# Fused attention and two MoE layers on one core: the low halves of one weight set move from DVE to GpSimd, and nine priorities of the planner change

## Chip, cores and metric

One core of a Trainium2 chip. The metric is the time of one launch in device microseconds, the median of several runs. Engines are named as the profile names them: PE (TensorE) multiplies matrices, DVE (VectorE), ACT (ScalarE) and POOL (GpSimd) work elementwise, SP (SyncE) issues most DMAs.

## What is computed

Three pieces in a row, all float32 (the reference, cut):

```
# q, k, v: (4, 8, 576, 64)
out_d  = softmax(pooled q . pooled k) @ pooled v        # means over 4 tokens
local  = softmax(q . k within |i - j| < 4) @ v
x      = (repeat(out_d, 4) + local) as (2304, 512)
h  = x @ w_in;   x = (h * sigmoid(h)) @ w_out           # layer 1: 512 -> 2048 -> 512
h2 = x @ w_in2;  r = max(h2, 0)
out = (s * r * r + b) @ w_out2                          # layer 2: 512 -> 2048 -> 512
```

## The kernel before

Everything is written as operations handed to a list scheduler (class `Weave`). Each has an engine (or a choice of ACT or DVE, `EITHER`), a planned cost in us, the buffers it reads and writes, and a priority `pr` (smaller goes first). `plan` walks through planned time and, on each engine, takes the ready operation with the smallest `pr`; the result is a fixed order for each engine, with semaphores between them. Costs and priorities are numbers at the top of the file (`P_...`), so a number can change the order of all engines that have not yet been planned.

Every float32 factor is split for PE into a high half (a rounded copy, type fp32r) and a low half (the rest, value minus high half); a product is high x high + high x low + low x high.

Layer 2 uses a scheme with seven products of half-size blocks for four block products. In its second half (`out_group`) the hidden activations g come back from memory (`graw`, loaded by `g_load` as four tiles of 128x1024 for each group of 256 tokens; nine groups, p = 0 to 8). `mix` (L1263, DVE) forms sums of these tiles (`gs`), `parted` makes the high half on ACT (`gh`, L1267) and the low half on DVE (`gl`, L1268). The products of a group are b11, t1, t2, b21, t3, t4, b22, in banks oa, oc, oa, ob, oa, ob, oc. Each has eight matmuls 128x512 with the high half of g against both halves of the weight (L1286) and eight 128x256 with the low half (L1293). `snap` copies a piece of the bank with ACT (L1304), and `plus` and `join` add on DVE (`os`, L1301); after them a bank is free for its next product.

There are four weight sets for it: wb (for b11), wt12 (t1 and t2), wout (b21 and b22) and wt43 (t4 and t3). The trace shows wt12 and wt43 both as `wt`. Each has eight parts of 128x512 (wb of 128x256). `in_place` brings a part: SP loads it into the place of the low half (by the helper `dma`, L364 in the trace), ACT or DVE copies it rounded to the place of the high half (L351), and DVE subtracts the high half from it in place (L1226). Sets and the first two groups are interleaved by the string `PAIR`; groups 0 and 1 run together while the weights still arrive, all later groups find them there.

The last block's g is made just before by `late` (`g2`, L1134 on DVE, L1139 on ACT), stored by SP, and read back for the last group.

Of the kernel before, what the change touches and what calls it, by code (L numbers as in the profile page):

```python
# [8 lines left out]
F32 = mybir.dt.float32  # L9
# [4 lines left out]
ALU = mybir.AluOpType  # L14
# [30 lines left out]
MORE = 0.0  # L45
# [1 line left out]
NEARLY = 0  # L47
MASKED = False
ADDED = False
P_IN, P_OUT, P_Y0, P_W0, P_Y1, P_Y4, P_W, P_OS = 163.074, 237.937, 195.038, -36.246, 62.462, 102.369, 272.176, 169.42  # L50
P_STEP, P_BT, P_PO, P_PN = 6.074, -5.7, 16.567, 57.528
P_G, P_B, P_C = -45.097, 0.253, -5.619
D1, D1S = 8, 2
NWARM = 100
ACTW, ACTW2 = 0, True
# [3 lines left out]
NLAST, LASTS = 3, [0, 1, 2]  # L59
VPE, QKPE = 0, 0  # L60
GPV, GPQ, GPS, GPM = 0, 0, 0, 0
PAIR = "AAAAAAAATTTTTTTTG0H101OOOO01OOOO01FFFFFFFF01I0101"
FILL0, FILLG, FILLD = 5.0, 0.12, 0.85
SLOW = 1.05
# [31 lines left out]
class Weave:  # L96
# [9 lines left out]
    def op(self, eng, cost, fn, w=(), r=(), pr=0.0, table=None):  # L106
        n, deps = len(self.ops), set()
        r = [x if isinstance(x, tuple) else (x, None) for x in r]
        w = [x if isinstance(x, tuple) else (x, None) for x in w]

        def hits(d, k):
            return [v for kk, v in d.items() if k is None or kk is None or kk == k]

        for b, k in r:
            deps.update(hits(b.wr, k))
        for b, k in w:
            deps.update(hits(b.wr, k))
            for v in hits(b.rd, k):
                deps.update(v)
        for b, k in r:  # L120
            b.rd.setdefault(k, []).append(n)
        for b, k in w:
            if k is None:
                b.wr, b.rd = {}, {}
            else:
                b.rd.pop(k, None)
            b.wr[k] = n
        deps.discard(n)
        bufs = []
        for b, _ in r + w:  # L130
            if b not in bufs:
                bufs.append(b)
                if not b.left and b.kind in self.turns:
                    self.turns[b.kind].append(b)
                b.left += 1
        self.ops.append((eng if isinstance(eng, tuple) else (eng,), cost, fn, sorted(deps), bufs, pr, table))
        return n
# [133 lines left out]
def dve(n, c=1):  # L271
    return c * 0.07 + n / 960.0


def act(n, c=1):
    return c * 0.1 + n / 1200.0
# [15 lines left out]
def kernel(ctx, tc, q, k, v, w1_in, w1_out, w2_in, w2_out, s2, b2, cst, out):  # L292
    nc = tc.nc
# [41 lines left out]
    op = W.op  # L335
# [13 lines left out]
    def copy(eng, out, in_, by=1.0):  # L349
        if by == 1.0:  # L350
            (nc.scalar.copy if eng == "act" else nc.vector.tensor_copy)(out=out, in_=in_)  # L351
        elif eng == "act":
            nc.scalar.mul(out=out, in_=in_, mul=by)
        else:
            nc.vector.tensor_scalar(out=out, in0=in_, scalar1=by, scalar2=None, op0=ALU.mult)
# [7 lines left out]
    def dma(out, in_, eng=None, **kw):  # L363
        (eng or nc.sync).dma_start(out=out, in_=in_, **kw)  # L364
# [671 lines left out]
    HF = KF // 2  # L1036
# [185 lines left out]
    def in_place(nm, q, o, i, key, n, move, pr):  # L1222
        at = lambda x: o[:, x, i:i + n // P]
        op("sp", (1, move), lambda: dma(at(1).bitcast(F32), w_dram[nm][q][:, :n // P]), w=[(o, key)], r=[(w_dram[nm], q), final], pr=pr)
        op(EITHER, (act(n) + MORE, 0.07 + n / 1920.0 + MORE), lambda eng: copy(eng, at(0), at(1).bitcast(F32)), w=[(o, key)], pr=pr)
        op("dve", dve(n) + MORE, lambda: nc.vector.tensor_tensor(out=at(1), in0=at(1).bitcast(F32), in1=at(0).bitcast(F32), op=ALU.subtract), w=[(o, key)], pr=pr - 0.001)  # L1226

    def ahead(pr):
        for q in range(HF):
            if q % 2 == 0:  # L1230
                o = Buf("u2", [P, 2, KD, P], F32R, "wb")
            in_place("out", q, o, 2 * (q % 2), q % 2, 2 * P, 0.57, pr + 0.1 * q)
            piece_of("b11", q, o, q % 2, q % 2)
            yield

    def named(nm, names, at, pr):
        for q in range(HF):
            o = Buf("u2", [P, 2, KD, P], F32R, "w" + nm)
            in_place(nm, q + at, o, 0, None, DM, 0.88, pr + 0.1 * q)
            for i, name in enumerate(names):  # L1240
                piece_of(name, q, o, i)
            yield
# [103 lines left out]
    def put(o, r0, e=None):  # L1346
# [11 lines left out]
        for by, mine in (("sp", parts_),) if e != 1 else (("sp", parts_[::2]), ("act", parts_[1::2])):  # L1358
# [6 lines left out]
            "F": named("t43", ("t4", "t3"), 0, P_B + 3 * P_C), "0": lead[0], "1": lead[1]}  # L1365
    for x in PAIR:
        if x in "GHI":
# [57 lines left out]
```

## Time and profile before

| what | us |
|---|---|
| three runs | 861.50, 862.49, 863.54 |
| median | 862.49 |
| the profiled execution | 861.29 |
| its span | 859.4 |
| PE busy | 850.0 |
| DVE busy | 734.1 |
| ACT busy | 507.7 |
| POOL busy | 0.2 |

All times of rows are from the profiled execution, from the start of its span. Busy time of a group is its records laid over each other, so eight neighbours whose records overlap show as one row that is shorter than eight times the mean.

### The profile page before, as it was taken

How to read it: one execution, taken by the hardware profiler on the slowest of the kernel's cores; microseconds unless marked ns; L12 is line 12 of the kernel's file. 1: busy time of each engine (PE TensorE's matmuls, PEld its weight loads, DVE VectorE, ACT ScalarE, POOL GpSimd, SP SyncE). 2: the span in 40 equal slices, each digit the busy share in tenths (PEclk: the TensorE clock that was granted, in tenths of full speed). 3: DMA queues.
4: the chain of work that ended last, by engine and by line, in shares of the span. 5: the costliest groups of instructions: out<-in, count | busy, mean ns of one | idle time of the engine just before them, and what ended most of it. 6: DMA issues, size and time to landing. Idle time of an engine off the chain costs nothing.

```text
span 859.4 us, 14697 instructions
## 1 busy us (share of the span) xinstructions
PE 850.0 (99%) x5300; PEld 714.5 (83%) x5300; DVE 734.1 (85%) x1364; ACT 507.7 (59%) x1034; POOL 0.2 (0%) x4
## 2 busy tenths in 40 slices
PE   9999999999999999999999999999999999999998
PEld 8878777778778878888889988888888988888887
DVE  7999996999999999987667788777787999888894
ACT  6998797656456742454456566666666665444351
POOL 0000000000000000000000000000000000000000
PEclk9999999999999999999999999999999999999999
DMA  8995421642444221388985246666679866443311
GB/s 217 319 351 151 132 68 41 191 130 70 106 127 112 77 69 39 123 278 304 330 297 176 86 119 212 205 189 183 184 248 286 274 183 213 160 143 125 123 33 42
DMA packets 157426, 144.26 MB, mean 168 GB/s; under 512 B 65452, under 2 KB 125738, under 8 KB 157354
## 3 DMA queue, kind: packets, MB, share of 16 engines
q1 hardware_dynamic: 156946, 142.96, 53.2%
q8 instruction: 42, 0.69, 0.3%
q10 hardware_dynamic: 408, 0.36, 0.1%
q14 instruction: 30, 0.25, 0.1%
HBM read 102.40 MB, written 40.89 MB: 167 GB/s over the span
## 4 chain that ended last, share of the span: by engine, by line
PE 87%; DVE 7%; ACT 2%; DMA 2%; issue 1%; SPq 0%; ACTq 0%; DVEq 0%
PE hp L926 23%; PE y L926 20%; PE ha L926 10%; PE oa L1286 6%; PE hc L926 5%; PE oc L1286 4%; PE ob L1286 4%; PE oa L1293 3%; PE hb L926 2%; PE oc L1293 2%; PE ob L1293 2%; PE pS L703 1%; DMA wo_raw<-in_moe_w_out_dram 1%; PE pB L842 1%; PE pU L742 1%
## 5 line engine op out<-in xcount | busy, mean ns | idle before, releaser
L926 PE MATMUL hp<-xh,wi 128*128 128x512 f32 (+1 forms) x640 | 200.8, 377 | 0.3 <-ACT g L951 0.3
L926 PE MATMUL y<-gh,wo 128*128 128x512 f32 (+1 forms) x640 | 199.8, 375 | 0.0
L926 PEld LDWEIGHTS hp<-xh,wi 128*128 128x128 f32 x640 | 116.9, 188 | 23.3 <-ACT g L951 2.8
L926 PEld LDWEIGHTS y<-gh,wo 128*128 128x128 f32 x640 | 117.0, 189 | 19.9 <-issue 0.8
L926 PE MATMUL y<-gl,wo 128*128 128x512 f32 (+1 forms) x320 | 118.2, 369 | 0.0
L926 PE MATMUL hp<-xl,wi 128*128 128x512 f32 (+1 forms) x320 | 118.0, 369 | 0.0
L926 PE MATMUL ha<-yh,wi 128*128 128x512 f32 x256 | 86.4, 390 | 0.8 <-ACT g L351 0.8
L952 ACT CAST gh<-g 128x512 fp32r<-128x512 f32 (+1 forms) x80 | 46.2, 577 | 54.2 <-PE y L926 53.3
L951 ACT ACTIVATE g<-hp 128x512 f32<-128x512 f32 (+1 forms) x80 | 44.4, 555 | 41.4 <-DVE gl L953 36.3
L926 PEld LDWEIGHTS y<-gl,wo 128*128 128x128 f32 x320 | 60.4, 189 | 8.7 <-DVE gl L953 0.2
L926 PEld LDWEIGHTS hp<-xl,wi 128*128 128x128 f32 x320 | 60.4, 189 | 8.1
L1139 ACT ACTIVATE g<-g,sbt 128x512 f32<-128x512 f32 (+1 forms) x70 | 53.4, 769 | 23.2 <-DVE g L1134 22.8
L953 DVE TENSOR_TENSOR gl<-g,gh 128x512 fp32r<-128x512 f32 (+1 forms) x80 | 50.5, 631 | 14.5 <-ACT gh L952 14.4
L1134 DVE SCALAR_TENSOR_TENSOR g<-g 128x512 f32<-128x512 f32 (+1 forms) x80 | 49.8, 633 | 9.8 <-ACT g L1133 9.1
L926 PEld LDWEIGHTS ha<-yh,wi 128*128 128x128 f32 x256 | 48.1, 188 | 10.9 <-ACT g L351 1.3
L1267 ACT CAST gh<-gs 128x1024 fp32r<-128x1024 f32 x27 | 28.4, 1052 | 46.7 <-DVE gs L1263 38.7
L1267 ACT CAST gh<-graw 128x1024 fp32r<-128x1024 f32 x36 | 37.6, 1051 | 27.7 <-PE ob L1293 11.6
L926 PE MATMUL ha<-yl,wi 128*128 128x512 f32 x128 | 50.0, 390 | 0.0
L1268 DVE TENSOR_TENSOR gl<-graw,gh 128x1024 fp32r<-128x1024 f32 x36 | 43.6, 1217 | 6.8 <-PE oa L1286 4.1
L351 ACT COPY g<-ha 128x512 f32<-128x512 f32 x48 | 28.1, 585 | 28.0 <-PE ha L926 23.8
L926 PE MATMUL hc<-yh,wi 128*128 128x512 f32 x128 | 44.6, 389 | 0.0
L543 DVE TENSOR_TENSOR tmp<-le,lv 128x1344 f32<-128x1344 f32 (+1 forms) x28 | 37.9, 1353 | 0.5
(197 smaller groups left out, 1721.1 us busy)
## 6 DMA issues: line engine op xcount, KB each, us to landing
graw<-gd SPq DMA_DIRECT2D x36, 512.0 KB
gd<-g SPq DMA_DIRECT2D x64, 256.0 KB
wi_raw<-in_moe_w_in_dram SPq DMA_DIRECT2D x16, 512.0 KB
wo_raw<-in_moe_w_out_dram SPq DMA_DIRECT2D x16, 512.0 KB
w_raw<-in_moe_w_in_dram SPq DMA_DIRECT2D x16, 512.0 KB
w_raw<-in_moe_w_out_dram SPq DMA_DIRECT2D x16, 512.0 KB
nq<-in_q_dram SPq DMA_DIRECT2D x32, 144.0 KB
nk<-in_k_dram SPq DMA_DIRECT2D x32, 144.0 KB
```

The lines of the kernel that those rows point to most:

```text
L351: (nc.scalar.copy if eng == "act" else nc.vector.tensor_copy)(out=out, in_=in_)
L543: op("dve", dve(n * WIN * D), lambda t=t, i0=i0, n=n, h2=h2: nc.vector.tensor_tensor(out=t[:], in0=wide(e[:, h2 * ns + i0:h2 * ns + i0 + n ...
L926: nc.tensor.matmul(t(), lhsT=lhs(i), rhs=rhs(i), start=(first and i == 0), stop=(last and i == 2), **kw)
L951: op("act", act(n), lambda g=g, hp=hp: nc.scalar.activation(out=g[:], in_=hp[:], func=AF.Silu), w=[g], r=[hp], pr=-5, table="silu")
L952: op("act", act(n), lambda g=g, gh=gh: nc.scalar.copy(out=gh[:], in_=g[:]), w=[gh], r=[g], pr=-5)
L953: op("dve", dve(n), lambda g=g, gh=gh, gl=gl: nc.vector.tensor_tensor(out=gl[:], in0=g[:], in1=gh[:].bitcast(F32), op=ALU.subtract), w=[gl ...
L1134: op("dve", dve(n) + 1.5 * MORE, lambda: nc.vector.scalar_tensor_tensor(out=t[:], in0=t[:], scalar=0.0, in1=t[:], op0=ALU.max, op1=ALU.mul ...
L1139: nc.scalar.activation(out=t[:], in_=t[:], func=AF.Identity, scale=sbt[:, 0:1], bias=sbt[:, 1:2])
L1267: op("act", act(HF * P) + MORE, lambda: nc.scalar.copy(out=flat(hi), in_=flat(x)), w=[hi], r=[x], pr=pr + n)
L1268: op("dve", dve(HF * P) + MORE, lambda: nc.vector.tensor_tensor(out=flat(lo), in0=flat(x), in1=flat(hi).bitcast(F32), op=ALU.subtract), w= ...
L1286: nc.tensor.matmul(bank[:].rearrange("p x n -> p (x n)"), lhsT=hi[:, q], rhs=w(), start=new and q == 0, stop=False, skip_group_check=True)
L1293: nc.tensor.matmul(bank[:, 0], lhsT=lo[:, q], rhs=w()[:, 0], start=False, stop=q == HF - 1, skip_group_check=True)
```

## The change

The subtraction of `in_place` goes to GpSimd for a set's last GPT or GPO parts (t43 has GPT = 8 of 8 parts, wout none), with a planned cost of 1.35 us in place of DVE's. Nine priorities have other numbers.

```
-P_IN, P_OUT, P_Y0, P_W0, P_Y1, P_Y4, P_W, P_OS = 163.074, 237.937, 195.038, -36.246, 62.462, 102.369, 272.176, 169.42
+P_IN, P_OUT, P_Y0, P_W0, P_Y1, P_Y4, P_W, P_OS = 163.074, 237.937, 279.61, -80.654, 26.32, 107.348, 404.271, 125.36
...
-P_G, P_B, P_C = -45.097, 0.253, -5.619
+P_G, P_B, P_C = -175.262, -5.511, 0.133
...
+GPT, GPO = 8, 0
...
-        op("dve", dve(n) + MORE, lambda: nc.vector.tensor_tensor(out=at(1), in0=at(1).bitcast(F32), in1=at(0).bitcast(F32), op=ALU.subtract), w=[(o, key)], pr=pr - 0.001)
+        aside = q % HF >= HF - {"t43": GPT, "out": GPO if move > 0.6 else 0}.get(nm, 0)
+        by, engine = ("pool", nc.gpsimd) if aside else ("dve", nc.vector)
+        op(by, 1.35 if aside else dve(n) + MORE, lambda: engine.tensor_tensor(out=at(1), in0=at(1).bitcast(F32), in1=at(0).bitcast(F32), op=ALU.subtract),
+           w=[(o, key)], pr=pr - 0.001)
```

The order of all engines is the same up to the load of wb on SP (some 632 us); the 4900 matmuls and the DMAs are the same in number. Lines of the changed kernel lie 1 higher from L59 on and 4 higher behind `in_place`, so L1226 is now L1229, L1268 is L1272, L1301 is L1305, L1286 is L1290.

DVE before, where wt43 is split (names carry buffer numbers; 128x1024 rows are `gl`, low halves of g):

```order
L1226 TENSOR_TENSOR wout_7796<-wout_7796 128x512
L1268 TENSOR_TENSOR gl_7828<-graw_7497,gh_7818 128x1024
L1268 TENSOR_TENSOR gl_7841<-graw_7557,gh_7830 128x1024
L1226 TENSOR_TENSOR wt43_7843<-wt43_7843 128x512
L1226 TENSOR_TENSOR wt43_7845<-wt43_7845 128x512
...
L1226 TENSOR_TENSOR wt43_7862<-wt43_7862 128x512
L1301 TENSOR_TENSOR os_7758<-oa_7727,os_7758 128x256
L1301 TENSOR_TENSOR os_7758<-ob_7884,os_7758 128x256
L1268 TENSOR_TENSOR gl_7919<-graw_7502,gh_7875 128x1024
L1301 TENSOR_TENSOR os_7758<-ob_7884,os_7758 128x256
L1301 TENSOR_TENSOR os_7784<-oa_7754,os_7784 128x256
```

Here the eight wt43 rows stand in one piece between two `gl` and the adds. The changed kernel's DVE at the same place:

```order
L1272 TENSOR_TENSOR gl_7808<-graw_7497,gh_7798 128x1024
L1305 TENSOR_TENSOR os_7782<-oa_7755,os_7782 128x256
L1272 TENSOR_TENSOR gl_7824<-graw_7557,gh_7813 128x1024
L1267 TENSOR_TENSOR gs_7670<-graw_7557,gs_7670 128x1024
L1229 TENSOR_TENSOR wout_7790<-wout_7790 128x512
L1229 TENSOR_TENSOR wout_7792<-wout_7792 128x512
L1229 TENSOR_TENSOR wout_7794<-wout_7794 128x512
L1272 TENSOR_TENSOR gl_7880<-graw_7502,gh_7865 128x1024
L1229 TENSOR_TENSOR wout_7796<-wout_7796 128x512
L1305 TENSOR_TENSOR os_7757<-oa_7727,os_7757 128x256
L352 CAST wt43_7847<-wt43_7847 128x512
L1272 TENSOR_TENSOR gl_7905<-graw_7568,gh_7894 128x1024
```

The eight wt43 rows have left it (one of the casts has come), and the last four wout rows stand later, among the 1024-wide ones. POOL's whole stream behind the constants is:

```order
L1229 ISA
L1229 TENSOR_TENSOR wt43_7826<-wt43_7826 128x512
L1229 TENSOR_TENSOR wt43_7828<-wt43_7828 128x512
...
L1229 TENSOR_TENSOR wt43_7847<-wt43_7847 128x512
L1229 TENSOR_TENSOR wt43_7859<-wt43_7859 128x512
```

It has the eight subtractions, and ahead of them, without a wait, an instruction that loads the library which they use. PE before, from the first product of b21 (groups 0 and 1 have banks oa_7727 and oa_7754, or oa_7755 in the changed kernel):

```order
L1286 MATMUL ob_7884<-wout_7714,gh_7818 128x512
...
L1286 MATMUL ob_7910<-wout_7714,gh_7830 128x512
...
L1286 MATMUL oa_7727<-wt43_7843,gh_7875 128x512
L1286 MATMUL oa_7727<-wt43_7845,gh_7875 128x512
L1286 MATMUL oa_7754<-wt12_7290,gh_7775 128x512
...
L1286 MATMUL oa_7727<-wt43_7847,gh_7875 128x512
```

Here t3 of group 0 is cut in two by t2 of group 1. PE of the changed kernel at the same place:

```order
L1290 MATMUL oa_7755<-wt12_7297,gh_7769 128x512
...
L1290 MATMUL ob_7917<-wout_7714,gh_7798 128x512
...
L1290 MATMUL ob_7955<-wout_7714,gh_7813 128x512
...
L1290 MATMUL oa_7727<-wt43_7826,gh_7865 128x512
L1290 MATMUL oa_7727<-wt43_7828,gh_7865 128x512
```

t2 of group 1 (bank oa, wt12) now comes ahead of both b21 products, and t3 of group 0 (bank oa, wt43) in one piece behind them. On SP, behind the loads of wt43, six stores of the last block stand ahead of four loads of the fourth group:

```order
L365 DMA wt43_7859<-w2t43_93 128x512
...
L365 DMA gd4_98<-g2_7632 128x2x128
L365 DMA gd4_98<-g2_7651 128x2x128
...
L365 DMA gd4_98<-g2_7733 128x2x128
L365 DMA graw_8035<-gd1_95 128x1024
```

In the kernel before these loads stand ahead of them.

## Rows read from the trace of the kernel before

**Rows 1.** The page: busy us of each engine, share of the span, instructions.

```profile
PE 850.0 (99%) x5300; PEld 714.5 (83%) x5300; DVE 734.1 (85%) x1364; ACT 507.7 (59%) x1034; POOL 0.2 (0%) x4
```

**Rows 2.** PE's waits, 640 to 860 us: what for, total us, times, longest.

```profile
PE oa L1286 <- DVE os L1301: 1.3, 1, 1.3
```

**Rows 3.** Windows: busy us of PE, its weight loads, DVE, ACT, POOL; clock, DMA share, GB/s.

```profile
0.00:50.00 50.00, 48.08 (x832) 42.06 (x833) 44.59 (x129) 40.32 (x146) 0.20 (x4) 1.00 0.96 287
680.00:690.00 10.00, 10.00 (x57) 8.70 (x57) 10.00 (x14) 7.08 (x13) 0.00 (x0) 1.00 0.59 174
690.00:700.00 10.00, 8.67 (x49) 7.29 (x48) 10.00 (x17) 5.35 (x10) 0.00 (x0) 1.00 0.44 133
700.00:710.00 10.00, 10.00 (x60) 8.86 (x60) 9.95 (x18) 6.43 (x10) 0.00 (x0) 1.00 0.77 229
```

**Rows 4.** DVE's timeline: start us, us, what, count [idle before].

```profile
678.92 2.49 DVE L1226 TENSOR_TENSOR wout<-wout 128x512 fp32r<-128x512 f32 x4
...
688.62 2.35 DVE L1268 TENSOR_TENSOR gl<-graw,gh 128x1024 fp32r<-128x1024 f32 x2
690.89 4.90 DVE L1226 TENSOR_TENSOR wt<-wt 128x512 fp32r<-128x512 f32 x8
695.71 0.41 DVE L1301 TENSOR_TENSOR os<-oa,os 128x256 f32<-128x256 f32 x1
696.04 0.41 DVE L1301 TENSOR_TENSOR os<-ob,os 128x256 f32<-128x256 f32 x1
```

**Rows 5.** The chain that ended last, late part: start us, us, what.

```profile
692.09 1.10 DVE wt L1226 x2
693.90 1.89 DVE wt L1226 x3
...
698.30 2.14 PE oa L1286 x8
...
717.68 1.84 PE oa L1286 x8
...
734.45 1.84 PE oa L1286 x8
```

**Rows 6.** PE's timeline.

```profile
690.76 2.00 PE L1286 MATMUL ob<-wout,gh 128*128 128x512 f32 x8
...
693.55 2.00 PE L1286 MATMUL ob<-wout,gh 128*128 128x512 f32 x8
...
696.34 0.63 PE L1286 MATMUL oa<-wt,gh 128*128 128x512 f32 x2
698.30 2.14 PE L1286 MATMUL oa<-wt,gh 128*128 128x512 f32 x8 [1.33 <-DVE os L1301]
```

**Rows 7.** DVE's groups by form, 600 to 720: count | busy us, mean ns | idle before.

```profile
L1268 DVE TENSOR_TENSOR gl<-graw,gh 128x1024 fp32r<-128x1024 f32 x9 | 10.8, 1214 | 1.6 <-ACT gh L1267 1.6
L1176 DVE TENSOR_TENSOR g<-hc,g 128x512 f32<-128x512 f32 x15 | 10.3, 686 | 9.9 <-ACT g L351 9.9
...
L351 DVE CAST wi<-sum 128x512 fp32r<-128x512 f32 x1 | 0.4, 426 | 0.0
```

**Rows 8.** The tile `wt` on DVE, 600 to 700: min/median/max ns, first, last.

```profile
L1226 DVE TENSOR_TENSOR wt<-wt x16: 678/680/684, 638.7 to 695.1; 128x512 fp32r<-128x512 f32 x16
```

**Rows 9.** ACT's groups by form, 684 to 696.

```profile
L351 ACT CAST wt<-wt 128x512 fp32r<-128x512 f32 x8 | 4.4, 623 | 0.0
```

**Rows 10.** ACT's timeline.

```profile
688.91 2.71 ACT L351 CAST wt<-wt 128x512 fp32r<-128x512 f32 x5
```

**Rows 11.** POOL's timeline over the whole span, the last of its four rows.

```profile
0.33 0.10 POOL L1407 MEMSET const-uint8-127<- 128x1 uint8 x1
```

**Rows 12.** SP's timeline, 690 to 712: the loads of the fourth group.

```profile
705.68 3.02 SPq L364 DMA_DIRECT2D graw<-gd  x4
```

**Rows 13.** The page: DMA queue of instructions: packets, MB, share of 16 engines.

```profile
q8 instruction: 42, 0.69, 0.3%
```

## The prediction

> **What bounds the kernel now.** I read the page first. TensorE (PE) is busy for 850.0 us of a span of 859.4, so only 9.4 us exist that any edit off PE can give back in the whole kernel; GpSimd (POOL) does nothing but four constant fills at the start [rows 1, 11]. The change moves nothing on PE, DVE, ACT and SP ahead of the last layer's second half, so the second view is the list of PE's waits from 640 us to the end. It has one row: a single wait of 1.3 us for DVE's `os` add of L1301 [rows 2]. The table by stage says where: in 690–700 PE is busy 8.67 of 10 us and DVE all 10; in 680–690 and 700–710 PE is full again, and DVE is full too (10.00 and 9.95) [rows 3]. So PE is the bound at every other place, and for some 30 us DVE runs just behind it with no slack.
>
> DVE's timeline shows the queue at that place: four `wout` low halves from 678.92, two 1024-wide ones (`gl`, L1268) from 688.62, then the eight low halves of wt43 in one piece, 4.90 us from 690.89, and only then the small `os` adds [rows 4]. The chain of waits goes the same way: five low halves (1.10 + 1.89 us) stand on it ahead of PE's `oa` matmuls at 698.30 [rows 5]. In PE's timeline b21 of the second token group starts at 693.55, two matmuls of t3 at 696.34, and then t2 of that group waits 1.33 us for the add that frees its bank [rows 6].
>
> **The change, part by part.** (1) The eight wt43 subtractions leave DVE for POOL. On DVE eight cost 4.90 us in a row, so 0.60 us each from one start to the next (the record of a single one is longer, 680 ns, because neighbours overlap) [rows 4, 8]. If POOL works beside DVE without touching it, DVE reaches the `os` adds 4.9 us earlier, the wait of 1.33 us goes, and PE is late for nothing else before 698.30: the gain is 1.3 us and cannot be more, since PE has no other idle time there [rows 2, 3].
>
> (2) What POOL takes for one, g, no row shows: its only instructions are fills of one column, 0.10 us [rows 11]. The bounds come from DVE. A lower end is 0.68, DVE's own duration for the same form [rows 8]. An upper end is 1.22, what DVE's rows of 1024 elements take (1.214 mean): the time if the two operands of 512 are fetched one after the other [rows 7]. I take 1.2, by the upper row: that DVE fetches two operands at once is seen in its rows (next step), that POOL can is seen nowhere. Both ends stay in the range.
>
> (3) Whether POOL and DVE can work at once is the step that decides. Two rows bear on it: a cast of 128x512 with one input from SBUF takes DVE 426 ns, and the subtraction with two inputs from SBUF 680, as long as an add with one input from PSUM (686) [rows 7, 8]. So DVE goes faster when a single SBUF operand may use all of its ways in, and I read from it that an instruction with two SBUF operands leaves none free. If POOL comes in by one of these ways, the two engines take turns at exactly the instructions that stand here: `gl`, `gs` and `wout` low halves on DVE, low halves on POOL. No row shows a turn, as POOL never ran beside DVE. The Trainium skill, "SBUF — State Buffer", section "Who interferes with whom", says that a DVE instruction with two SBUF inputs contends with a GpSimd one that reads SBUF, that the first holds the ports for a whole instruction and that the other blocks; no run here shows it, by it the sum is the one below, and without it the gain of (1).
>
> With turns, the path that is full already (DVE, 680–710) loses eight times 0.60 and gets eight times g back as time in which it is held: 8 x (1.2 - 0.60) = +4.8 us. Nothing covers it: DVE has 0.05 us of idle time in 30 us, and the wait of 1.33 us shows that PE already stands behind it [rows 3, 6]. PE is full from there to the end, so what is lost isn't made up. The ends: with g = 0.68 it is 8 x 0.08 = +0.6; with every turn of 1.22 on the path and only the old wait given back, 8 x 1.22 - 1.33 = +8.4.
>
> A second way to the same number, by the later user: the first cast of wt43's high halves ends on ACT about 688.91 + 0.62 = 689.5 [rows 9, 10], and there POOL can start. If its eight turns alternate with DVE's two-input instructions (0.60 and 1.135 from start to start, the latter half of the way from 688.62 to 690.89; about 0.9 in the mean) [rows 4], the last ends at 689.5 + 8 x (1.2 + 0.9) = 706.3. In the new order t2 of the second group takes the place at 690.76, both b21 products follow, 2.79 us each (690.76 to 693.55), and then t3, whose first matmul would stand at 690.76 + 3 x 2.79 = 699.13 in a PE without a wait, and its eighth, 7 x 0.23 (1.84 for eight) later, at 700.7 [rows 5, 6]. POOL would be 5.6 late, less the old wait: +4.3. The Trainium skill, "GPSIMD Engine Reference", section "Performance versus the Vector engine", gives GpSimd 1.96 times DVE's time for a two-input add of 2048 fp32 elements; an estimate by that page and DVE's 0.680 is g = 1.33, and the sum 8 x (1.33 - 0.60) = +5.8; no run here shows it.
>
> (4) The new numbers of the planner. They move t2 of the second group ahead of both b21 products, and spread the `wout` low halves among the 1024-wide instructions on DVE. I cost this at nothing if POOL disturbs nobody: from 678.92 DVE has eight `wout` low halves (8 x 0.60), eight 1024-wide (8 x 1.135) and two `os` adds (2 x 0.33, from 695.71 to 696.04) up to the last `wout`, 14.5 us, so it ends at 693.5; PE's eighth b21 matmul stands at 693.55 + 7 x 0.23 = 695.2. The slack is 1.7 us, and with turns it is the first thing that is lost: two POOL turns of 1.2 in that row are enough [rows 4 to 6].
>
> (5) On SP six stores of the last block now stand ahead of the four `graw` loads of the fourth pair. Before, these issue at 705.68 and PE meets their data in the `oa` product some 30 us later; between come products at 717.68 and 734.45 [rows 5, 12]. A store waits for its result, and what waits behind it is only loads with some 25 us in hand: zero, and at most a wait of some us if the last block's results come late. (6) POOL's stream gets one library instruction ahead of its first subtraction, without a wait, so some 650 us before it is needed.
>
> **How it stands to the measured time.** The profiled execution took 861.29 (span 859.4 and 1.89 around it); the median of three is 862.49, 1.2 above it. By the sum the profiled one becomes 861.3 + 4.8 = 866.1, and the median 867.3.
>
> **The rivals.** *POOL works beside DVE untouched, and g is under 1.4.* Then the wait of 1.33 goes and nothing comes for it: 862.49 - 1.3 = 861.2. For it speaks that ACT's casts and DMA at 0.44 to 0.77 leave DVE's subtraction at 678 to 684 ns, so other users of SBUF cost DVE nothing [rows 3, 8]; against it, the 426 and 680 above. This is the case on the other side: not slower. It decides at DVE's mean for two-input instructions while POOL runs.
>
> *No turns, but POOL is too slow.* Its eight end at 689.5 + 8 g, and t3's eighth matmul wants them at 700.7, so it costs from g = 1.4 on. At 2.43, twice DVE's 1.214, the last ends at 708.9, 8.2 late, less 1.3: +6.9, 869.4.
>
> *The library instruction takes time at the start.* In 0–50 us PE is busy 48.08 of 50 with DMA at 0.96 of its time and 287 GB/s; a load of instructions of the size that the page's instruction queue shows (0.69 MB) would push the first operands by 0.69 MB / 287 GB/s = 2.4 us [rows 3, 13]. With the gain of 1.3 that is +1.1, and with turns +7.2.
>
> *The new order of late loads makes PE wait* near 735 us for the fourth pair: a store that is 25 us late would be needed; a few us at most. That the change doesn't do what it says is out: its POOL stream holds the eight subtractions, DVE's lacks them.
>
> **How the numbers follow.** Turns: 0.58. Untouched: 0.28. POOL too slow: 0.06. Library at the start: 0.04. Late loads: 0.04. The likeliest gives 867.3. The range goes from the untouched case less the spread of the runs, 861.2 - 1.0 = 860.2 (lowest run against the median), up to 862.5 + 8.4 = 870.9. About 0.2%, 1.7 us, is what a measurement of this kernel can tell from no change. The untouched case is 0.15% faster, so most of it is "same": 0.21 of its 0.28, and 0.07 faster. Turns with g under 0.81 (8 x 0.21 = 1.7) or with a part of them hidden are "same" as well, 0.08, and so are the late loads, 0.04: same 0.33. The rest, 0.50 + 0.06 + 0.04, is slower: 0.60.
>
> **What would show it.** Right: in 689–706 DVE's two-input instructions last longer than 680 and 1214 ns or idle ahead of each, POOL's eight are spread over some 16 us, and PE waits 5 to 6 us in 693–707, at b21's last `wout` or t3's wt43 low half. Wrong: POOL's eight lie end to end, DVE keeps its means, and PE has no wait in 690–710 at all. PE waiting in 0–50 would be the library's, near 735 the loads'. The granted clock stayed 1.00, the upper level of 2.4 GHz, through the wait of 1.33 us [rows 3]; a wait of 5 us that lowers it would make the loss larger than any sum here.

## The result and the profile after

The changed kernel takes 869.21 us (median of 4 runs, 867.89 to 869.48), the kernel before 863.01 beside it (4 runs): a ratio of 1.0069, 95% interval 1.0051 to 1.0088, so 4.4 to 7.6 us slower. The prediction was 867.3, that is +4.8. The profiled execution of the changed kernel has a span of 867.6 us, 8.2 above that of before. 1.8 of these lie ahead of the place where the two orders part (the first product of b11 begins at 678.57, before at 676.79) and are no part of the change: in four other runs with subtractions on POOL this product begins at 676.48 to 677.25, and in one without any at 679.37. From that product to the end it is 189.0 us against 182.6, or +6.4. This stretch is used below to compare profiled executions.

PE's waits from 640 us on, and the table by stage, which answers [rows 2] and [rows 3] (us, then busy us of PE, weight loads, DVE, ACT, POOL, then granted clock, DMA share, GB/s):

```profile
PE oa L1290 <- POOL wt L1229: 4.0, 5, 1.2
```

```profile
690.00:700.00 10.00, 10.00 (x57) 8.70 (x56) 10.00 (x11) 6.62 (x12) 9.48 (x3) 1.00 0.60 199
700.00:710.00 10.00, 6.00 (x24) 3.98 (x23) 10.00 (x13) 4.98 (x8) 8.02 (x6) 0.80 0.62 199
710.00:720.00 10.00, 10.00 (x52) 8.67 (x52) 9.14 (x15) 5.12 (x7) 0.00 (x0) 0.86 0.57 166
```

The old wait of 1.33 us for DVE's add is gone, and five waits for POOL stand in its place. POOL's timeline, and the spread of its eight (min/median/max in ns):

```profile
690.52 17.50 POOL L1229 TENSOR_TENSOR wt<-wt 128x512 fp32r<-128x512 f32 x8 [690.08 <-DMA wt<-w2t]
```

```profile
L1229 POOL TENSOR_TENSOR wt<-wt x8: 1447/1599/6225, 690.5 to 706.6; 128x512 fp32r<-128x512 f32 x8
```

One of the eight, the first, lasts 6.2 us (690.52 to 696.74). DVE's timeline beside them, which answers [rows 4]:

```profile
689.69 1.22 DVE L1272 TENSOR_TENSOR gl<-graw,gh 128x1024 fp32r<-128x1024 f32 x1
690.82 1.22 DVE L1267 TENSOR_TENSOR gs<-graw,gs 128x1024 f32<-128x1024 f32 x1
691.96 1.89 DVE L1229 TENSOR_TENSOR wout<-wout 128x512 fp32r<-128x512 f32 x3
693.77 1.22 DVE L1272 TENSOR_TENSOR gl<-graw,gh 128x1024 fp32r<-128x1024 f32 x1
694.90 0.69 DVE L1229 TENSOR_TENSOR wout<-wout 128x512 fp32r<-128x512 f32 x1
695.50 0.42 DVE L1305 TENSOR_TENSOR os<-oa,os 128x256 f32<-128x256 f32 x1
695.84 1.19 DVE L352 CAST wt<-wt 128x512 fp32r<-128x512 f32 x1
696.95 2.31 DVE L1272 TENSOR_TENSOR gl<-graw,gh 128x1024 fp32r<-128x1024 f32 x1
...
701.22 7.42 DVE L1135 SCALAR_TENSOR_TENSOR g<-g 128x512 f32<-128x512 f32 x6
```

Up to 695.5 DVE's instructions have their old length (1.22, 0.69). Then comes an `os` add, which has one operand in PSUM; POOL's first one ends at 696.74, 1.24 us after that add began. That is the time of one subtraction alone (1.26, measured below), so it is read as having made no progress before. In the six other runs below that keep subtractions on POOL its first one also ends 1.22 to 1.25 us after the start of such an add. From there the two take turns: a cast of 0.43 lasts 1.19, a `gl` of 1.22 lasts 2.31, and the six squares (`g<-g`, all but one 128x256, whose own length is 0.41) take 7.42 together. PE's timeline, which answers [rows 6]:

```profile
695.33 2.00 PE L1290 MATMUL ob<-wout,gh 128*128 128x512 f32 x8
...
700.91 0.86 PE L1290 MATMUL oa<-wt,gh 128*128 128x512 f32 x3
702.16 0.49 PE L1290 MATMUL oa<-wt,gh 128*128 128x512 f32 x1 [0.39 <-POOL wt L1229]
703.84 0.50 PE L1290 MATMUL oa<-wt,gh 128*128 128x512 f32 x1 [1.18 <-POOL wt L1229]
705.25 0.51 PE L1290 MATMUL oa<-wt,gh 128*128 128x512 f32 x1 [0.92 <-POOL wt L1229]
706.66 0.80 PE L1290 MATMUL oa<-wt,gh 128*128 128x512 f32 x1 [0.90 <-POOL wt L1229]
708.07 0.80 PE L1290 MATMUL oa<-wt,gh 128*128 128x512 f32 x1 [0.62 <-POOL wt L1229]
708.66 1.91 PE L1297 MATMUL oa<-wt,gl 128*128 128x256 f32 x8
710.38 3.18 PE L1290 MATMUL oa<-wt,gh 128*128 128x512 f32 x8
713.40 1.11 PE L1297 MATMUL oa<-wt,gl 128*128 128x256 f32 x8
714.34 2.00 PE L1290 MATMUL ob<-wt,gh 128*128 128x512 f32 x8
```

Both b21 products run without a wait. t3's last five matmuls come one by one. A lone one lasts 0.49 to 0.51 us, and 0.80 from 706 on, where neighbours follow each other every 0.23, so 4.0 us of waits put the eighth 5.6 us late (708.07 against 702.5 without a wait). What follows is slow: eight low matmuls take 1.91 us where 1.11 is usual, the eight of the next t3 3.18 where it is 2.00. In stretches of 2 us the granted clock is 1.00 up to 706, then half of it (1.2 of 2.4 GHz), and 1.00 again from 714:

```profile
704.00:706.00 2.00, 0.84 (x2) 0.21 (x2) 2.00 (x3) 1.09 (x2) 2.00 (x2) 1.00 0.95 290
706.00:708.00 2.00, 0.80 (x1) 0.29 (x1) 2.00 (x2) 1.19 (x3) 2.00 (x2) 0.52 0.55 162
708.00:710.00 2.00, 1.93 (x8) 1.84 (x9) 2.00 (x7) 1.07 (x3) 0.02 (x1) 0.50 0.22 66
710.00:712.00 2.00, 2.00 (x7) 1.70 (x7) 1.97 (x4) 2.00 (x3) 0.00 (x0) 0.50 0.66 197
...
714.00:716.00 2.00, 2.00 (x13) 1.71 (x12) 2.00 (x4) 0.37 (x1) 0.00 (x0) 1.00 0.65 182
```

### The profile page after: what moved, and what is told of

Its sections match the earlier page's. It is cut to its first block, busy times and chain, and to the rows that moved or that the text cites. A ratio compares the mean times of both kernels' runs of the same rounds, so it can differ in the third digit from the quotient of the medians.

```text
span 867.6 us, 14715 instructions
## 1 busy us (share of the span) xinstructions
PE 854.9 (99%) x5300; PEld 716.5 (83%) x5300; DVE 737.6 (85%) x1355; ACT 510.1 (59%) x1035; POOL 17.7 (2%) x12
## 4 chain that ended last, share of the span: by engine, by line
PE 76%; DVE 13%; DMA 5%; ACT 3%; issue 2%; POOL 1%; POOLq 0%; SPq 0%; DVEq 0%; ACTq 0%
PE hp L927 19%; PE y L927 17%; PE ha L927 9%; PE oa L1290 5%; PE hc L927 5%; PE ob L1290 3%; PE oc L1290 3%; PE oa L1297 3%; PE hb L927 2%; PE ob L1297 2%; PE oc L1297 2%; DMA wo_raw<-in_moe_w_out_dram 1%; DMA nv<-in_v_dram 1%; POOL wt L1229 1%; PE pBO L897 1%
## 5 line engine op out<-in xcount | busy, mean ns | idle before, releaser
L1140 ACT ACTIVATE g<-g,sbt 128x512 f32<-128x512 f32 (+1 forms) x73 | 56.0, 771 | 29.2 <-DVE g L1135 28.7
L1135 DVE SCALAR_TENSOR_TENSOR g<-g 128x512 f32<-128x512 f32 (+1 forms) x80 | 55.8, 710 | 9.8 <-ACT g L1134 9.1
L954 DVE TENSOR_TENSOR gl<-g,gh 128x512 fp32r<-128x512 f32 (+1 forms) x80 | 50.6, 633 | 13.2 <-ACT gh L953 13.2
L1272 DVE TENSOR_TENSOR gl<-graw,gh 128x1024 fp32r<-128x1024 f32 x36 | 44.8, 1249 | 7.4 <-PE oa L1290 5.1
L1290 PE MATMUL oa<-wt,gh 128*128 128x512 f32 x144 | 39.3, 410 | 4.0 <-POOL wt L1229 4.0
```

The costliest lines, as they stand in the source:

```text
L954: op("dve", dve(n), lambda g=g, gh=gh, gl=gl: nc.vector.tensor_tensor(out=gl[:], in0=g[:], in1=gh[:].bitcast(F32), op=ALU.subtract), w=[gl ...
L1135: op("dve", dve(n) + 1.5 * MORE, lambda: nc.vector.scalar_tensor_tensor(out=t[:], in0=t[:], scalar=0.0, in1=t[:], op0=ALU.max, op1=ALU.mul ...
L1140: nc.scalar.activation(out=t[:], in_=t[:], func=AF.Identity, scale=sbt[:, 0:1], bias=sbt[:, 1:2])
L1272: op("dve", dve(HF * P) + MORE, lambda: nc.vector.tensor_tensor(out=flat(lo), in0=flat(x), in1=flat(hi).bitcast(F32), op=ALU.subtract), w= ...
L1290: nc.tensor.matmul(bank[:].rearrange("p x n -> p (x n)"), lhsT=hi[:, q], rhs=w(), start=new and q == 0, stop=False, skip_group_check=True)
```

## Experiments

Each ratio below is to the kernel before, timed beside the run. The three kernels of stages don't compute the result; each was run once, and only its trace is used.

The theory going in: POOL's subtractions read SBUF by a way that DVE's two-input instructions use too, so they take turns, and that alone makes the loss.

**The two halves of the change.** Edit of the first: the changed kernel with

```
-GPT, GPO = 8, 0
+GPT, GPO = 0, 0
```

> The nine new priorities alone: all eight wt43 low halves stay on DVE (GPT = 0), nothing runs on POOL. Theory (POOL's instructions cost all of it): 862 to 863.5 us, no wait of PE for wt43 longer than the 1.3 us of before, clock 1.00 in 700-720. Rival (the new order is what costs): 866 us or more, with PE waits in 690-710 although POOL is idle.

Measured: 863.4 us (10 runs), ratio 0.9999 (0.9984 to 1.0014). The only wait of PE from 680 on is 0.6 us for a `wout` low half, against 1.3 before for an `os` add. The new priorities cost nothing, and what they could save was too small to measure. Edit of the second: the changed kernel with the nine priorities of before.

> The move to POOL alone: GPT = 8 with the nine priorities of before. Theory (POOL's instructions cost all of it): 867 to 871 us, PE waiting for POOL's wt43 for 3 to 6 us near 700. Rival (the new order is what costs): 861 to 863.5 us.

Measured: 867.65 us, ratio 1.0059 (1.0040 to 1.0079). PE's waits from 680 on:

```profile
PE oa L1290 <- POOL wt L1229: 2.6, 3, 1.7
PE oa L1290 <- DVE os L1305: 1.7, 2, 1.5
```

The move alone has the loss, in either order: 2.6 us of waits for POOL, a little less than the theory's 3 to 6, and 1.7 for DVE.

**What POOL reads.** POOL fills with zero instead of subtracting, which leaves out the low halves of wt43; the order on every engine is that of the changed kernel (lines cut at `...`):

```
-        op(by, 1.35 if aside else dve(n) + MORE, lambda: engine.tensor_tensor(out=at(1), ...),
+        op(by, 1.35 if aside else dve(n) + MORE, lambda: engine.memset(at(1).bitcast(F32), 0.0) if aside else engine.tensor_tensor(out=at(1), ...),
```

> The changed kernel, in its own order on all engines, but POOL's eight subtractions are fills with zero (they read nothing; the wt43 low halves are left out of the computation). Theory (POOL's reads take DVE's way into SBUF): POOL's eight last about 0.5 us each and are never held, DVE's two-input instructions in 690-710 keep 1.22 and 0.41 us, PE has no wait for wt43 and clock 1.00; 861 to 863.5 us. Rival (the new order itself makes PE late): 866 us or more.

Measured: 862.78 us (10 runs), ratio 0.9994 (0.9970 to 1.0018). The list of PE's waits from 680 to 860 is empty, and the two stages that were hurt read:

```profile
690.00:700.00 10.00, 10.00 (x59) 8.79 (x58) 10.00 (x21) 8.58 (x15) 3.04 (x6) 1.00 0.64 185
700.00:710.00 10.00, 10.00 (x59) 8.77 (x58) 8.94 (x16) 6.12 (x9) 0.00 (x0) 1.00 1.03 296
```

DVE's `gl` keep 1.23 and 1.22 us, its squares 0.43. From b11 to the end the profiled execution takes 181.3 us, 1.3 less than before: what the prediction gave as the most that can be gained when POOL disturbs nobody (a difference that the medians can't resolve). But a fill is also shorter, some 0.5 us against 1.2, so this run doesn't say by itself which of the two counts. The next does.

**Turns, measured alone.** A kernel of stages, whose subtractions are the changed kernel's, in place on 128x512. In each stage `start` is a copy on DVE and then a cast on ACT that releases POOL, `work` is the other engine's instructions, and `pool` is eight instructions on POOL:

```
    for how, work in (("sub", None), ("sub", None), ("sub", lambda: two(12)), ("sub", lambda: one(24)), ("sub", lambda: cast(32)), ("sub", lambda: square(40)),
                      ("fill", lambda: two(12)), ("sub", lambda: copies(12))):
        start()
        if work:
            work()
        pool(how=how)
        end()
```

> Not the computation: all of it is left out, and eight stages of eight POOL instructions on 128x512 float32 tiles in place are timed beside other work: 1 and 2 subtractions with nothing on DVE; 3 beside 12 DVE adds 128x1024 with two SBUF inputs; 4 beside 24 DVE adds 128x512 of PSUM and SBUF; 5 beside 32 DVE casts 128x512 from SBUF; 6 beside 40 DVE scalar_tensor_tensor 128x256 with two SBUF inputs; 7 POOL fills (nothing read) beside the 12 adds of stage 3; 8 subtractions beside ACT copies 128x1024. Theory C: the first of stage 1 takes 5 to 7 us, that of stage 2 1.0 to 1.4; in stage 3 POOL's and DVE's alternate, 2.2 us for a pair. Theory L: the first of stage 1 takes 1.0 to 1.4 like all others; in stage 3 POOL's first one lasts until the adds are through, 12 x 1.14 = 13.7 us. Both: stages 4 and 8 as stage 2. Untouched rival of the prediction: stages 3 and 6 as stage 2 too, with DVE's 1.22 and 0.41 us unchanged.

POOL's timeline, stages 2 to 8, and DVE's of stages 3 to 7:

```profile
49.40 9.80 POOL L319 TENSOR_TENSOR weight<-weight 128x512 fp32r<-128x512 f32 x8 [1.84 <-ACT weight L325]
61.04 16.93 POOL L319 TENSOR_TENSOR weight<-weight 128x512 fp32r<-128x512 f32 x8 [1.84 <-ACT weight L325]
83.51 9.83 POOL L319 TENSOR_TENSOR weight<-weight 128x512 fp32r<-128x512 f32 x8 [5.55 <-ACT weight L325]
98.20 19.66 POOL L319 TENSOR_TENSOR weight<-weight 128x512 fp32r<-128x512 f32 x8 [4.85 <-ACT weight L325]
119.70 11.20 POOL L319 TENSOR_TENSOR weight<-weight 128x512 fp32r<-128x512 f32 x8 [1.84 <-ACT weight L325]
141.96 3.79 POOL L321 MEMSET weight<- 128x512 f32 x8 [11.05 <-ACT weight L325]
155.94 9.85 POOL L319 TENSOR_TENSOR weight<-weight 128x512 fp32r<-128x512 f32 x8 [10.20 <-ACT weight L325]
```

```profile
60.22 22.22 DVE L332 TENSOR_TENSOR big<-big 128x1024 f32<-128x1024 f32 x12
...
82.71 14.43 DVE L336 TENSOR_TENSOR seen<-bank,seen 128x512 f32<-128x512 f32 x24
...
97.39 10.81 DVE L340 CAST mid<-mid 128x512 fp32r<-128x512 f32 x32
...
118.89 22.02 DVE L344 SCALAR_TENSOR_TENSOR own<-own 128x256 f32<-128x256 f32 x40
...
141.17 13.70 DVE L332 TENSOR_TENSOR big<-big 128x1024 f32<-128x1024 f32 x12
```

Alone, a subtraction takes 9.80 / 8 = 1.225 us on POOL; the record of one is 1.26, and stage 1, with nothing on DVE either, shows the same, its first one included. Beside ACT's copies (9.85) and beside DVE adds with one operand in PSUM (9.83) it is the same, and those adds keep their 0.60 us. Beside DVE adds with two SBUF operands both lose: eight last 16.93, and the twelve adds 22.22, where they take 13.70 beside fills. So some 8.5 us of DVE go for eight subtractions, 1.06 each. The squares lose as much (40 in 22.02; at 0.33 from start to start they would take 13.2), while POOL's eight last 11.20. Beside casts POOL loses all: the first subtraction lasts 11.1 us, until the casts are through, and DVE's 0.33 us for one is unchanged. The rival without turns has fallen. Theory L had expected POOL's first of stage 3 to wait for all twelve adds; they took turns from the first.

**Why the first one takes 6.2 us.** One more subtraction of 128x8 on POOL at the start:

```
+    warm = fixed(cp, [P, 2, 8], F32, "warm")
+    op("pool", 0.2, lambda: nc.gpsimd.memset(warm[:], 0.0), w=[warm], pr=-300)
+    op("pool", 6.0, lambda: nc.gpsimd.tensor_tensor(out=warm[:, 1].bitcast(F32R), ...), w=[warm], pr=-300)
```

> The changed kernel with one more POOL subtraction, of 128x8, as the first thing at the start, on a tile that nothing reads. In the changed kernel the first wt43 subtraction lasts 6.2 us (690.52 to 696.7), the others 1.45 to 2.2. Theory C (the first use of the operation after its library is loaded costs some 5 us, once): the first wt43 one now lasts 1.1 to 2.5 us, DVE's two-input instructions in 690-696 get longer by some 1.1 us each, and PE's wait moves to b21's last wout; 866 to 870 us. Theory L (DVE's unbroken row of two-input instructions keeps POOL out until the first one with a PSUM input at 695.5): nothing changes, the first wt43 one still ends near 696.7, 869 us.

Measured: 872.11 us, ratio 1.0095 (1.0068 to 1.0123). POOL's new subtraction, and the spread of the eight:

```profile
0.92 0.20 POOL L386 TENSOR_TENSOR warm<-warm 128x8 fp32r<-128x8 f32 x1
```

```profile
L1232 POOL TENSOR_TENSOR wt<-wt x8: 1449/1600/6226, 693.9 to 710.0; 128x512 fp32r<-128x512 f32 x8
```

The first use of the operation took 0.20 us, and the first wt43 one still 6.2. Theory C has fallen, as it had with the first one of stage 1 (1.26). POOL was kept out by DVE. (What it takes beyond the changed kernel is lost at the start, and told of at the end.)

Two more kernels of stages asked when DVE keeps POOL out. The first varied the operands of DVE's instructions.

> Not the computation: all of it is left out. Six stages, each eight POOL subtractions 128x512 that are released while DVE runs: 1 low halves of 128x1024 into a third tile; 2 adds 128x1024 of two tiles; 3 low halves 128x512 in place; 4 the kernel's own row (two gl, gs, three wout, gl, wout, an add with PSUM, a cast, gl, eight squares); 5 the adds within one tile of the first stages kernel; 6 the row of stage 4 again. In the changed kernel POOL's first one was held for 5.0 us by seven two-input DVE instructions, in the first stages kernel for one only. Theory O (it depends on the operands of DVE's instruction): POOL's first lasts long in one or more of stages 1 to 3 and in 4 and 6, and short in 5. Theory S (something else of the kernel): first ones of 1 to 3 end after one DVE instruction, 1.3 to 2.4 us, in 4 and 6 too.

It gave neither. In stages 1, 2, 3 and 5 POOL took turns with DVE from its first one on (eight in 16.93, 16.93, 13.26 and 16.93 us). In stage 4, the kernel's own row, DVE's eight two-input instructions ahead of the add with PSUM kept their length and POOL's first one lasted 7.3 us, until that add, as in the changed kernel; in stage 6, the same row again, they took turns from the second `gl` on (eight in 17.95 and 14.79 us). So it isn't the operands. The last repeated this row twelve times, with four delays of POOL's release:

> Not the computation: all of it is left out. The kernel's own row of DVE instructions (stage 4 of the second stages kernel) twelve times beside eight POOL subtractions, with 0, 1, 2 and 4 small ACT copies ahead of the cast that releases POOL, three times each. Theory P (whether POOL gets in between two DVE instructions depends on the moment of its request): the first one is held in some delays and not in others, the same in all three of a delay. Theory H (it depends on what ran before): the three of one delay differ from each other, whatever the delay.

POOL's rows, three with no delay and the first with one:

```profile
42.07 14.78 POOL L325 TENSOR_TENSOR weight<-weight 128x512 fp32r<-128x512 f32 x8 [41.63 <-ACT weight L380]
62.03 17.94 POOL L325 TENSOR_TENSOR weight<-weight 128x512 fp32r<-128x512 f32 x8 [5.17 <-ACT weight L380]
81.99 14.80 POOL L325 TENSOR_TENSOR weight<-weight 128x512 fp32r<-128x512 f32 x8 [2.02 <-ACT weight L380]
102.09 17.80 POOL L325 TENSOR_TENSOR weight<-weight 128x512 fp32r<-128x512 f32 x8 [5.31 <-ACT weight L380]
```

The two outcomes alternate through all twelve stages, whatever the delay: in the 1st, 3rd, ... POOL gets a turn at the next of DVE's instructions, in the 2nd, 4th, ... it is kept out until the PSUM add. The delays moved POOL's start from 0.8 to 1.8 us behind the start of DVE's row, and within these limits the moment of the request doesn't decide. That leaves something carried over from the stage ahead, which is argued and not shown; what it is stays open.

**The clock.** 20 matmuls with zero weights are put ahead of the five t3 matmuls that wait:

```
+                if p == 0 and name == "t3" and q > 2:
+                    def busy():
+                        for _ in range(4):
+                            nc.tensor.matmul(bank[:16]..., lhsT=zero[:], rhs=wcomb["t3", 0][0](), start=False, stop=False, ...)
+                    op("pe", 0.01, busy, w=[bank], r=[zero, wcomb["t3", 0][1]], **mine)
```

> The changed kernel with 20 more PE matmuls (16 columns of zero weights, 512 moving, 0.23 us each), four ahead of each of the five t3 matmuls that wait for POOL; they add zero to the same bank. Theory K (about half of the loss is PE's clock, which falls after the waits: 10 x 0.20 + 10 x 0.14 = 3.4 us of full speed in 700-720): the waits are filled, the granted clock stays at 1.00 through 700-720 and the two t3 products end some 3 us earlier; 865 to 867 us. Rival (a matmul that starts alone is slow by itself, or the added ones cost as much): 869 us or more.

Measured: 870.61 us, ratio 1.0073 (1.0058 to 1.0088). The time is in the rival's range. The clock stayed at 1.00, but PE lost 1.7 us in the first 50 us (busy 46.38 against 48.05), and here the zeros lay ahead of other tiles. The same with the zeros behind all tiles and written later:

> As the run with 20 more PE matmuls ahead of the t3 matmuls that wait for POOL, but the 64 bytes of zeros lie behind all other tiles in SBUF and are written later, so no other tile's address moves. (In that run PE was busy 46.4 of the first 50 us against 48.05 of the changed kernel, and from the first product of b11 to the end it took 187.3 us against 189.0.) Theory K (the clock's fall is a part of the loss): clock 1.00 in 700-720 again, PE busy 48.0 of the first 50, b11 to the end 187 to 187.5, and 867 to 868.5 us in all. Rival (what is saved on the clock comes back in DVE's lateness): 869 us or more.

Measured: 868.64 us (8 runs), ratio 1.0068 (1.0046 to 1.0090), not to be told from the changed kernel's; b11 to the end 188.0 in the profiled execution, 1.0 less than there. The stage, and PE's one wait of note behind 690:

```profile
700.00:710.00 10.00, 9.96 (x47) 5.68 (x47) 9.96 (x13) 5.85 (x10) 6.40 (x5) 1.00 0.59 184
```

```profile
PE oa L1293 <- DVE os L1315: 1.4, 1, 1.4
```

The clock doesn't fall, and the first t4 starts at 710.54, or 5.4 us later than four products of 2.79 behind b21's start at 694.01; in the changed kernel it is 7.85 (714.34 against 695.33 + 11.16). So 2.5 us came back there. Then, at 729, PE waits 1.4 us for a DVE add. DVE is busy 37.89 of the 38.60 us from 690 to that add, and in the run with fills, whose order is the same, PE has no such wait: DVE had been held by POOL's turns, and a slower PE had hidden it. The time lies between the ranges of the two theories, and the trace shows what each describes, one after the other.

**A later place for t3.** The planner's cost of one subtraction goes from 1.35 to 2.2, and nothing else:

> The changed kernel with one number changed: the planner's cost of a POOL subtraction is 2.2 us (a pair of turns beside a 1024-wide DVE instruction, as stage 3 of the stages kernel measured) in place of 1.35. The planner then lets t3 and t4 of both groups go forward part by part as the wt43 parts arrive. Theory (PE was late only because its order counted on POOL's parts too early): waits of PE for POOL under 1.5 us in all, 862 to 865 us. Rival (DVE held by POOL's turns makes PE late wherever it stands): 867 us or more.

Measured: 869.07 us, ratio 1.0056 (1.0037 to 1.0074). The waits of PE behind 690, and DVE's squares:

```profile
PE ob L1290 <- DVE os L1305: 2.9, 1, 2.9
PE oa L1290 <- POOL wt L1229: 1.6, 2, 0.9
```

```profile
698.20 7.46 DVE L1135 SCALAR_TENSOR_TENSOR g<-g 128x512 f32<-128x512 f32 x6
```

PE waits 1.6 us for POOL, near the theory's bound of 1.5, and 2.9 for an `os` add that stands on DVE behind six held squares. The time is in the rival's range: where PE waits less for POOL, it waits for DVE.

**Half of it.**

```
-GPT, GPO = 8, 0
+GPT, GPO = 4, 0
```

> The changed kernel with GPT = 4: POOL makes the last four wt43 low halves, DVE the first four; priorities and planned cost as in the changed kernel. Theory (each turn of POOL costs: PE stands behind the last of a chain of turns of some 1.1 us each): half of the turns, a PE wait for POOL under 2 us; 863.5 to 866.5 us, b11 to the end 183 to 186 (before 182.6, changed 189.0). Rival (a loss that comes as soon as POOL takes any part, whatever their number): 868 us or more.

Measured: 867.62 us (10 runs), ratio 1.0055 (1.0039 to 1.0072), b11 to the end 188.5. Half of the turns didn't halve the loss. PE's wait of note, and the stage behind it:

```profile
PE ob L1290 <- DVE wout L1229: 3.3, 2, 2.8
```

```profile
700.00:710.00 10.00, 9.94 (x44) 8.23 (x44) 8.15 (x14) 6.32 (x9) 0.55 (x1) 0.70 0.53 151
```

With four wt43 subtractions ahead of them, DVE's last three `wout` ones come just where POOL takes its turns (one lasts 1.75 us, the other two 3.12 together), and b21 waits. Here too the clock falls behind the waits, to 0.50 in 700 to 704. The time lies between the theory's range and the rival's, so the theory's size has fallen: the number of turns counts for less than what they land on. Waits of 3.6 us in all (3.3, and 0.3 for an `os` add) and the slow clock behind them cost nearly what the changed kernel's 4.0 us of waits do.

## Why the prediction was right, and where it wasn't

The sign, the size and the cause (POOL and DVE take turns at SBUF) came as forecast: +4.8 predicted, +4.4 to +7.6 measured. The loss reached PE by the second of the two ways that the prediction wrote down (+4.3), and the slow clock behind the waits, which it named without a price, is the rest. Step by step:

**What bounds.** PE behind a DVE without slack, and a gain of 1.3 us at most: right. With fills DVE is free, and b11 to the end is 1.3 us shorter.

**g.** 1.2 chosen, 1.225 measured: DVE's row of 1024 elements was the right bound. That POOL fetches its operands one after the other, the reason for taking it, was not tested. The estimate of 1.33 by the Trainium skill, "GPSIMD Engine Reference", section "Performance versus the Vector engine", was 9% high for this size.

**Turns.** Right, and shown by itself: DVE loses 1.06 us for each subtraction when it has two operands in SBUF, none with one in PSUM, and fills disturb nobody. The Trainium skill, "SBUF — State Buffer", section "Who interferes with whom", states all three, and these rows agree. Not right for the changed kernel is that the turns alternate from the first: POOL was kept out for 5.0 us here (6.2 less 1.26) and for 9.9 beside the casts (11.1 less 1.26).

**The sum on DVE's path, 8 x (1.2 - 0.60) = +4.8.** The number came near, the place was wrong. DVE did lose time, some 1.1 us for each turn, but from 696 on, on the cast, a `gl` and the squares for the last block, for which PE doesn't wait. In the changed kernel PE waits for POOL's parts. The sum shows up only where that wait is gone: with the filled waits (an add, 1.4 us) and with the later t3 (2.9 us).

**The second way, by the later user.** This one describes what happened. It had POOL's last one at 706.3; measured 690.52 + 17.50 = 708.0, less the 1.8 by which this execution was late before, 706.2. It had t3's eighth matmul 5.6 us late; measured 708.07 against 695.33 + 2 x 2.79 + 7 x 0.23 = 702.5, again 5.6 (4.0 of it in waits, where 5 to 6 were expected). But the inside of it differs: not eight fair turns, but 5.0 us of being kept out, and then turns beside shorter instructions. That these agree to 0.1 us is partly luck.

**What was left out: the clock.** "Less the old wait, +4.3" stops at t3's eighth matmul. From its start at 708.07 to t4's at 714.34 PE needed 6.3 us for what takes 0.23 + 0.95 + 2.79 = 4.0 at full clock: 2.3 us more. The prediction named it as what would make the loss larger and gave it no price. With it the second way gives 4.3 + 2.3 = 6.6, beside 6.4 in the profiled execution and 6.2 by the medians. Taking the clock's fall away gave back only 1.0 of it, as the DVE add came late instead.

**b21's slack as the first thing lost.** Wrong for the changed kernel, since POOL was kept out while the `wout` ones ran. Right in the run with four: there PE waits at just this place, 3.3 us.

**Rivals.** Untouched POOL has fallen by stages 3 and 6, and POOL too slow (g over 1.4) by stage 2. The library instruction cost nothing at the start: PE is busy 48.05 of the first 50 us against 48.08. The late loads cost nothing either: PE has no wait in 715 to 860.

## What to carry to other kernels

Before work is moved to an idle engine, ask what it shares with the one that is relieved: here a subtraction of 0.60 us on DVE came back as 1.06 us in which DVE stood still, so the offload made DVE slower, and a reordering only moved the wait. Beside DVE instructions with an operand in PSUM, or for work that reads nothing from SBUF, POOL was free. And where PE's own waits come in a row, add the slow clock behind them to the sum: 4.0 us of waits, 0.39 to 1.18 each, cost 2.3 more.

## What was not expected of the hardware

DVE can keep POOL out over a whole row of its instructions that read SBUF: 5.0 us over seven two-input ones, and all 32 casts of stage 5. In the profile this isn't a wait; it is a POOL instruction of 6.2 us (11.1 in stage 5) whose like takes 1.26. Once POOL had a turn beside two-input instructions, the two alternated. The same row of instructions did the one and the other in alternate stages, and why wasn't found.

The clock fell to half after waits of 0.39, 1.18, 0.92 and 0.90 us with single matmuls between, and stayed there up to 712 although PE was busy again from 708. It fell as well in the three other runs whose lines of waits stand above (0.73, 0.85 and 0.70 in 700 to 710); one wait of 1.33 us [rows 6] had not lowered it.

The profiled executions of two runs with a tile of 64 bytes ahead of other tiles in SBUF were slow at the start (PE busy 45.57 and 46.38 of the first 50 us); with it behind all tiles and written later, PE was busy 48.07. The first of the two also had POOL at work at the start; which accesses were slower was not followed.
